# Where the Mish of eight held chunks stands in ScalarE's queue, in a fused attention and two-layer MoE kernel

## The chip, the cores and the metric

The kernel runs on one core of a Trainium2 chip. The metric is the device time of one execution in microseconds: 1049.36 as the median of three runs (1048.75 to 1050.46). Everything below is read from one profiled execution of that kernel. Five engines work side by side, each with its own queue that it takes in order: TensorE (PE, with its weight loads as PEld), VectorE (DVE), ScalarE (ACT), GpSimd (POOL) and SyncE (SP), which issues the loads from memory.

## The reference

Three stages follow each other over 1152 tokens of width 512:

```
attn_out = softmax over 144 means of 4 positions (repeated 4 times) + softmax over a band of +-3 positions
x  = attn_out as [1152, 512]
h  = x @ w_in                      # 512 -> 2048
g  = h * tanh(log1p(exp(h)))       # Mish
x  = g @ w_out                     # 2048 -> 512
P  = exp(x @ w_gate - max), 8 rounds of row and column normalisation
out = sum over 8 experts of P[:, e] * (relu(x @ w1[e]) @ w2[e])
```

The change touches only the Mish of the second stage. All matmuls that matter are done as three products of rounded operands (high x high, low x high, high x low), so that every operand is first split into a rounded part and a rest.

## The kernel before, in words

The middle stage is cut into chunks. A chunk is 128 of the 2048 hidden columns for one of three groups of 384 tokens. `gemm1(s)` (L500) computes chunk s into a PSUM bank with 12 matmuls; `mish(s, hps)` (L489) then does three things: ACT applies Mish in place (L495), ACT copies the result rounded into `ghi` or a slot of `xform` (L496), and DVE subtracts to get the rest, `glo` (L497). `gemm2(s)` (L513) multiplies both by `w_out` with 12 matmuls, four chunks later (`LAG = 4`).

Eight of the chunks are computed early. While attention still runs, the first tokens are ready and PE has gaps; there `p_gemm1` (L931) puts the first matmuls of the eight chunks named in `HELD` (L942), and `hold` copies each result out of PSUM to a tile `ghi` or `glo` in SBUF (L953 on DVE, L955 on ACT). These chunks wait there; in the main loop (L1025) they are the numbers s = 6 to 9 (tiles `glo`) and 12 to 15 (tiles `ghi`). At their turn the loop does not call `gemm1` but `mish` alone (L1037 and L1038).

Three things set the order of the queues. In attention a planner (`Plan`) lays out the steps by a table of costs, and `pin` (L567) ties each instruction to the one ahead of it on its engine. The loop is traced after that; a scheduler places its instructions on each engine as early as its own timing allows, unless `tc.issue_after(x)` holds them back: what is traced inside such a block is queued behind x, if it is on x's engine. `last["pe"]` is the last matmul of the plan, `last["mish"]` the newest ACT copy (L496, or L855 in attention). Before the change the loop's `issue_after(last["pe"])` holds back only the work on PE. The Mish of a held chunk needs nothing but its SBUF tile, so nothing holds it back on ACT.

ACT evaluates functions from a loaded table, and Exp (attention, L721) and Mish (L495) are in different ones; an ACT_TABLE_LOAD stands wherever the queue goes from one to the other.

Other steps that the text names: L654 turns queries and keys on PE, L667 copies them on ACT; L745 and L810 are scores, L713 their maxima on DVE, L721 the exponentials on ACT, L727 to L731 the scaling on DVE, L763 and L828 transposes on PE with copies L766 and L830 on ACT, L781 and L838 the products with the values, L788 and L844 their joining, L855 and L857 the split of the result. Weights come as 64-bit numbers: loaded by SP (L436, L872), turned into 32 bits by ACT (L453, L891) and three steps on DVE (L454 to L457, L895 to L904), split by ACT (L463) and POOL (L464).

Of the kernel before, what the change touches and what calls it, by code (L numbers as in the profile page):

```python
# [325 lines left out]
def attn_moe_moe_kernel(  # L326
# [44 lines left out]
    def f32(a):  # L371
        return a.bitcast(F32)

    def new(pool, shape, dt, tag, bufs=2):
        return pool.tile(shape, dt, tag=tag, name=tag, bufs=bufs)
# [29 lines left out]
    def bank(tag):  # L405
        turn[tag] += 1
        return of_tag[tag][turn[tag] % 4]

    last = {}
# [30 lines left out]
    def w_raw():  # L440

        n, i = divmod(place["raw"], 2)
        if n >= len(ring) or n >= place["split"] + RAWB:
            return
        place["raw"] += 1
        if i == 0:
            wraw[n] = raw_place(n % RAWB)
        w = raw64.pop((n, i)).rearrange("p (n t) -> p n t", t=2)  # L450
        c = slice(512 * i, 512 * i + 512)
        lo, hi, x = w[:, :, 0], w[:, :, 1], wraw[n].bitcast(U32)[:, c]
        ACT.activation(out=f32(x), in_=f32(hi), func=AF.Copy, scale=F64_BIAS)  # L453
        DVE.tensor_scalar(out=x, in0=x, scalar1=3, scalar2=0x7FFFFFF8, op0=ALU.logical_shift_left,  # L454
                          op1=ALU.bitwise_and)
        DVE.scalar_tensor_tensor(out=x, in0=hi, scalar=0x80000000, in1=x, op0=ALU.bitwise_and, op1=ALU.bitwise_or)
        DVE.scalar_tensor_tensor(out=x, in0=lo, scalar=29, in1=x, op0=ALU.logical_shift_right, op1=ALU.bitwise_or)  # L457
        load_w64()
# [7 lines left out]
    def w_split():  # L466

        n = place["split"]
        place["split"] += 1
        kind, j = ring[n]  # L470
        hi, lo = (new(ap, [128, 1024], F32R, f"{z}{kind}", NBUF) for z in ("hi", "lo"))
        split(wraw.pop(n), hi, lo)
        whl[kind, j] = hi, lo

    def free_at(n):

        kind, j = ring[n]
        before = [x for k, x in ring[:n] if k == kind]
        if len(before) < NBUF:
            return 0  # L480
        return 2 * lasts[kind, before[-NBUF]] + 2 + (LAG if kind == 2 else 0)
# [6 lines left out]
    gq, acc, ysum, gl, held = {}, {}, {}, {}, {}  # L488
    def mish(s, hps):  # L489

        if s < SWITCH:
            ghi, glo = (xform[:, s % (LAG + 1), z].rearrange("p a b -> p (a b)")[:, 0:NMAX] for z in range(2))
        else:
            ghi, glo = (new(ap, [128, NMAX], F32R, z, LAG) for z in ("ghi", "glo"))
        ACT.activation(out=hps, in_=hps, func=AF.Mish)  # L495
        last["mish"] = ACT.activation(out=ghi, in_=hps, func=AF.Copy)  # L496
        DVE.tensor_tensor(out=glo, in0=hps, in1=f32(ghi), op=ALU.subtract)  # L497
        gq[s] = ghi, glo

    def gemm1(s):  # L500
        g, j, h, _, _ = chunks[s]
        n, c0 = groups[g][1] * TQ, groups[g][0] * TQ
        bk = bank("w")[:, 0:n]
        whi, wlo = (z.rearrange("p (a b) -> p a b", a=KD) for z in whl[1, j])
        o = slice(128 * h, 128 * h + 128)
        i = 0
        for kk in range(KD):
            for a, b in ((whi, xhi), (whi, xlo), (wlo, xhi)):
                PE.matmul(out=bk, lhsT=a[:, kk, o], rhs=b[:, kk, c0:c0 + n], start=(i == 0), stop=(i == 3 * KD - 1))  # L509
                i += 1  # L510
        mish(s, bk)

    def gemm2(s):  # L513
        g, j, h, first, end = chunks[s]
        n, c0 = groups[g][1] * TQ, groups[g][0] * TQ
        whi, wlo = (z.rearrange("p (a b) -> p a b", a=2) for z in whl[2, j])
        ghi, glo = gq.pop(s)
        done = end and s // 2 == last_of[g]
        joined = g in ysum
        if end and not joined:  # L520
            ysum[g] = room(g)
        for d in range(KD):
            if first:
                acc[d] = bank("acc")
            bk = acc[d][:, 0:n]
            o = slice(128 * d, 128 * d + 128)
            for i, (a, b) in enumerate(((whi, ghi), (whi, glo), (wlo, ghi))):
                PE.matmul(out=bk, lhsT=a[:, h, o], rhs=b, start=(first and i == 0), stop=(end and i == 2))  # L528
            if not end:
                continue  # L530
            z = ysum[g][d][:, 0:n]
            if not joined:
                ACT.activation(out=z, in_=bk, func=AF.Copy)
            elif not done:
                DVE.tensor_tensor(out=z, in0=bk, in1=z, op=ALU.add)
            else:
                y = xs[d // KH][:, d % KH, c0:c0 + n]
                DVE.tensor_tensor(out=y, in0=bk, in1=z, op=ALU.add)
                parts(y, xhi[:, d, c0:c0 + n], xlo[:, d, c0:c0 + n])
# [10 lines left out]
    def gate():  # L550

        gl["w"] = wghl = tp.tile([128, KD, 128], F32R, name="wghl")
        SP.dma_start(out=wg, in_=w_gate.rearrange("(a p) e -> p a e", p=128))
        ACT.activation(out=wghl, in_=ident.unsqueeze(1).to_broadcast([128, KD, 128]), func=AF.Copy, scale=0.0)
        ACT.activation(out=wghl[:, :, 0:NE], in_=wg, func=AF.Copy)
        DVE.tensor_tensor(out=wghl[:, :, NE:2 * NE], in0=wg, in1=f32(wghl[:, :, 0:NE]), op=ALU.subtract)
# [468 lines left out]
    for s in range(S0):  # L1025
        if s == S0 - 1:
            with tc.issue_after(last["mish"].ins):
                gate()
        n = place["raw"] // 2
        if n < len(ring) and s >= need[ring[n]] - AHEAD and (s % 2 == 0 or s >= need[ring[n]] - 4):  # L1030
            with tc.issue_after(last["mish"].ins):
                w_raw()
        n = place["split"]
        if n < len(ring) and 2 * n + 2 <= place["raw"] and free_at(n) <= s:
            w_split()
        with tc.issue_after(last["pe"]):
            if s in held:  # L1037
                mish(s, held.pop(s))  # L1038
            else:
                gemm1(s)  # L1040
            if s >= LAG:
                gemm2(s - LAG)

# [595 lines left out]
```

## Time and profile before

| | |
|---|---|
| median of three runs | 1049.36 us |
| the profiled execution | 1048.87 us |
| its span, from first to last instruction | 1046.9 us |
| PE busy | 1026.5 us, 98% of the span |
| DVE busy | 694.5 us, 66% |
| ACT busy | 536.0 us, 51% |
| POOL busy | 391.9 us, 37% |
| attention with the held chunks | from 0 to 120.66 us |
| main loop | from 120.66 us to about 263 us |
| last stage | from there to the end |

The shares are means over stages that have different limits. A timeline row begins with the start and the duration of a piece of work, and ends in brackets with how long its engine had been idle and what ended that. A row of the chain of waits is a piece of the path that was last to end.

### The profile page before, as it was taken

How to read it: one execution, taken by the hardware profiler on the slowest of the kernel's cores; microseconds unless marked ns; L12 is line 12 of the kernel's file. 1: busy time of each engine (PE TensorE's matmuls, PEld its weight loads, DVE VectorE, ACT ScalarE, POOL GpSimd, SP SyncE). 2: the span in 40 equal slices, each digit the busy share in tenths (PEclk: the TensorE clock that was granted, in tenths of full speed). 3: DMA queues.
4: the chain of work that ended last, by engine and by line, in shares of the span. 5: the costliest groups of instructions: out<-in, count | busy, mean ns of one | idle time of the engine just before them, and what ended most of it. 6: DMA issues, size and time to landing. Idle time of an engine off the chain costs nothing.

```text
span 1046.9 us, 17277 instructions
## 1 busy us (share of the span) xinstructions
PE 1026.5 (98%) x6376; PEld 933.8 (89%) x6376; DVE 694.5 (66%) x1338; ACT 536.0 (51%) x1365; POOL 391.9 (37%) x435
## 2 busy tenths in 40 slices
PE   8988899999999999999999999999999999999998
PEld 6876799999999888988998899989998999889997
DVE  6876654434478988776665776586756677657844
ACT  6999854434358544544553445435553455345531
POOL 0111122103045437744453444435452455244530
PEclk9998999999999999999999999999999999999999
DMA  9552222212003011201111012101110121011002
GB/s 220 162 129 66 70 91 100 91 72 71 1 1 121 22 50 61 61 2 59 61 61 32 29 61 61 54 8 61 61 61 1 61 61 61 14 48 61 21 1 91
DMA packets 47996, 63.40 MB, mean 61 GB/s; under 512 B 15272, under 2 KB 31656, under 8 KB 47912
## 3 DMA queue, kind: packets, MB, share of 16 engines
q1 hardware_dynamic: 47912, 62.30, 20.0%
q8 instruction: 50, 0.82, 0.3%
q14 instruction: 34, 0.28, 0.1%
HBM read 59.93 MB, written 2.36 MB: 59 GB/s over the span
## 4 chain that ended last, share of the span: by engine, by line
PE 90%; ACT 7%; DMA 2%; DVE 1%; issue 0%; DVEq 0%; ACTq 0%
PE bank L1554 38%; PE bank L1502 30%; PE bank L528 7%; PE bank L509 6%; PE bank L1179 2%; ACT pl L721 2%; PE bank L1161 2%; DMA raw<-in_moe_w_out_dram 1%; ACT pg L721 1%; ACT L495 1%; ACT L721 1%; PE bank L1334 1%; DMA rawq<-in_k_dram 0%; PE bank L654 0%; PE bank L1343 0%; PE bank L781 0%
## 5 line engine op out<-in xcount | busy, mean ns | idle before, releaser
L1517 ACT ACTIVATE xs<-bank 128x384 f32<-128x384 f32 x231 | 113.2, 492 | 258.1 <-PE bank L1502 238.5
L1554 PE MATMUL bank<-xs,hhi 128*128 128x512 f32 x760 | 235.7, 391 | 0.0
L1570 DVE SCALAR_TENSOR_TENSOR yacc<-bank,P,yacc 128x512 f32<-128x512 f32 (+1 forms) x217 | 161.0, 746 | 94.3 <-PE bank L1554 92.4
L1554 PEld LDWEIGHTS bank<-xs,hhi 128*128 128x128 f32 x760 | 140.5, 188 | 19.6
L1554 PE MATMUL bank<-xs,hlo 128*128 128x512 f32 x380 | 148.9, 392 | 0.0
L1477 POOL TENSOR_TENSOR wops<-wsums,wops 128x256 fp32r<-128x256 f32 x114 | 85.8, 762 | 163.2 <-ACT wops L1475 163.0
L1244 DVE TENSOR_TENSOR bank<-bank,xs 128x384 f32<-128x384 f32 x189 | 99.0, 559 | 45.7 <-ACT xs L1517 37.3
L1554 PE MATMUL bank<-wc,hhi 128*128 128x512 f32 x398 | 123.0, 390 | 0.0
L1502 PE MATMUL bank<-xform,wops 128*128 128x384 f32 x558 | 106.2, 335 | 0.0
L1502 PEld LDWEIGHTS bank<-xform,wops 128*128 128x128 f32 x558 | 98.0, 188 | 4.4
L464 POOL TENSOR_TENSOR lo<-raws,hi 128x512 fp32r<-128x512 f32 x26 | 34.3, 1327 | 167.8 <-ACT hi L463 154.9
L1322 DVE SCALAR_TENSOR_TENSOR hlo<-bank,hhi 128x384 fp32r<-128x384 f32 x150 | 78.8, 550 | 16.3 <-ACT hhi L1319 14.0
L1319 ACT ACTIVATE hhi<-bank 128x384 fp32r<-128x384 f32 x150 | 70.4, 487 | 37.1 <-DVE bank L1244 31.5
L1554 PEld LDWEIGHTS bank<-wc,hhi 128*128 128x128 f32 x398 | 74.5, 188 | 15.6
L1244 DVE TENSOR_TENSOR wsums<-raws 128x256 f32<-128x256 f32 x147 | 64.1, 448 | 35.4 <-POOL wops L1477 17.4
L1554 PEld LDWEIGHTS bank<-xs,hlo 128*128 128x128 f32 x380 | 71.3, 188 | 16.2
L1554 PE MATMUL bank<-wc,hlo 128*128 128x512 f32 x199 | 78.2, 393 | 0.0
L1477 POOL TENSOR_TENSOR ysum<-wsums,ysum 128x256 fp32r<-128x256 f32 x59 | 45.5, 777 | 81.3 <-ACT ysum L1475 81.2
L1502 PE MATMUL bank<-xhi,wops 128*128 128x384 f32 x252 | 70.8, 336 | 0.3 <-ACT xs L1517 0.3
L1475 ACT ACTIVATE wops<-wsums 128x256 fp32r<-128x256 f32 x114 | 45.3, 411 | 34.9 <-PE bank L1502 27.7
L1364 POOL TENSOR_TENSOR xs<-temp,xs 128x512 fp32r<-128x512 f32 x42 | 58.0, 1402 | 9.9 <-ACT xs L1362 9.9
L1502 PE MATMUL bank<-xform,ysum 128*128 128x384 f32 x282 | 54.9, 336 | 0.0
(237 smaller groups left out, 2185.6 us busy)
## 6 DMA issues: line engine op xcount, KB each, us to landing
temp<-in_moe_w_dram SPq DMA_DIRECT2D x64, 256.0 KB, 3.1
raws<-in_moe_w_dram SPq DMA_DIRECT2D x16, 768.0 KB, 4.5
raw<-in_moe_w_in_dram SPq DMA_DIRECT2D x16, 512.0 KB, 6.7
raw<-in_moe_w_out_dram SPq DMA_DIRECT2D x16, 512.0 KB, 3.2
raws<-in_moe_w_dram SPq DMA_DIRECT2D x5, 512.0 KB
rawq<-in_q_dram SPq DMA_DIRECT2D x4, 576.0 KB, 10.1
rawv<-in_v_dram SPq DMA_DIRECT2D x8, 288.0 KB
vw<-in_v_dram SPq DMA_DIRECT2D x12, 192.0 KB, 4.2
```

Of the source, the lines that this page charges most:

```text
L509: PE.matmul(out=bk, lhsT=a[:, kk, o], rhs=b[:, kk, c0:c0 + n], start=(i == 0), stop=(i == 3 * KD - 1))
L528: PE.matmul(out=bk, lhsT=a[:, h, o], rhs=b, start=(first and i == 0), stop=(end and i == 2))
L1244: eng.tensor_tensor(out=out, in0=a, in1=b, op=ALU.add if cb > 0 else ALU.subtract)
L1319: ACT.activation(out=hb.t[0], in_=bk.t[:, 0:TH], func=AF.Relu)
L1322: DVE.scalar_tensor_tensor(out=hb.t[1], in0=bk.t[:, 0:TH], scalar=0.0, in1=f32(hb.t[0]), op0=ALU.max, op1=ALU.subtract)
L1364: add("wlo", lambda raw=raw, y=y: POOL.tensor_tensor(out=y.t[:, 1], in0=raw(), in1=f32(y.t[:, 0]), op=ALU.subtract), r=[("r2", c), ("ch", ...
L1475: add("wh", lambda src=src, y=y: ACT.activation(out=y.t[:, 0], in_=piece(src), func=AF.Copy), r=key + rk, w=[("wh", r, n)] + wk, b=[y] + bs)
L1477: add("wl", lambda src=src, y=y: POOL.tensor_tensor(out=y.t[:, 1], in0=piece(src), in1=f32(y.t[:, 0]), op=ALU.subtract), r=key + [("wh", r ...
L1502: PE.matmul(out=bb.t[:, 0:TH], lhsT=y.t[:, wz, kk, :], rhs=x[xz][:, kk, :], start=(fresh and i == 0), stop=(i == 3 * KH - 1), skip_group_c ...
L1517: add("keep", lambda src=src, y=y: ACT.activation(out=y.t, in_=src.t[:, 0:TH], func=AF.Copy), r=[key, "late"], w=[("b", id(y))], b=[src, y])
L1554: PE.matmul(out=bk.t[:, a:b], lhsT=h[hz][:, js], rhs=y[:, wz, a:b], start=(f == fs[0] and i == 0), stop=(f == fs[-1] and i == 2))
L1570: DVE.scalar_tensor_tensor(out=y, in0=bk.t[:, a:b], scalar=p, in1=y, op0=ALU.mult, op1=ALU.add)
```

## The change

Inside the loop, the `mish` of a held chunk gets an `issue_after` of its own, on the copy (L496) of the chunk traced before it. The branches are swapped; what is computed stays.

```
         with tc.issue_after(last["pe"]):
-            if s in held:
-                mish(s, held.pop(s))
+            if s not in held:
+                gemm1(s)
             else:
-                gemm1(s)
+                with tc.issue_after(last["mish"].ins):
+                    mish(s, held.pop(s))
             if s >= LAG:
                 gemm2(s - LAG)
```

The queues of PE, DVE, POOL and SP keep their order, instruction for instruction. ACT's changes in three kinds of places. The first is in attention, at the exponentials L721 (tiles `pl` near, `pg` far); `ghi` is a held chunk:

```order
 L891 ACTIVATE raws<-raw_991 128x512
-L495 ACT_TABLE_LOAD
-L495 ACTIVATE ghi<-ghi 128x384
-L721 ACT_TABLE_LOAD
 L721 ACTIVATE pl_101,ld<-bank_115,lm 96x102 x4
 L721 ACTIVATE pg_103,gd<-bank_111,gm 72x144 x2
 L721 ACTIVATE pg_104,gd<-bank_117,gm 72x144 x2
-L495 ACT_TABLE_LOAD
-L495 ACTIVATE ghi<-ghi 128x384
-L721 ACT_TABLE_LOAD
```

A held Mish leaves, and with it the load of its table and the load of the exponentials' table behind it. In all, eleven loads leave attention with the eight Mishes: eight with the four `ghi`, two with the first `glo` and one with the second, behind which no exponential follows.

The second is the head of the loop on ACT, behind the last split of attention's result (L855):

```order
-L495 ACTIVATE glo<-glo 128x384
 L855 ACTIVATE xhi<-bank_112 128x4x96
 L453 ACTIVATE raws<-raw_1593 128x512
 L463 ACTIVATE hi_1776<-raws 128x512
+L495 ACT_TABLE_LOAD
 L495 ACTIVATE bank_113<-bank_113 128x384
 L496 ACTIVATE xform<-bank_113 128x384
```

One load now stands ahead of the loop's first Mish, that of chunk 0, and it takes over that Mish's wait for the matmuls of chunk 0.

The third is at the held chunks' turn in the loop, here s = 6 to 9 (the same again for 12 to 15, on `ghi`):

```order
 L453 ACTIVATE raws<-raw_1774 128x512
-L496 ACTIVATE xform<-glo 128x384 x2
+L495 ACTIVATE glo<-glo 128x384
+L496 ACTIVATE xform<-glo 128x384
+L495 ACTIVATE glo<-glo 128x384
+L496 ACTIVATE xform<-glo 128x384
 L463 ACTIVATE hi_1878<-raws 128x512
 L453 ACTIVATE raws<-raw_1816 128x512
```

Each held Mish now stands directly ahead of the copy that reads it.

## Rows read from the trace of the kernel before

**Rows 1.** The page's part 4: shares of the chain that ended last.

```profile
PE 90%; ACT 7%; DMA 2%; DVE 1%; issue 0%; DVEq 0%; ACTq 0%
```

**Rows 2.** Busy time by stretch: PE, PEld, DVE, ACT, POOL, clock, DMA.

```profile
66.74:90.80 24.06, 16.40 (x211) 12.73 (x207) 14.15 (x43) 23.84 (x66) 0.00 (x0) 0.96 0.07 16
90.80:97.00 6.20, 6.20 (x67) 5.62 (x68) 2.19 (x6) 5.08 (x20) 1.27 (x1) 0.60 0.30 89
97.00:120.66 23.66, 19.86 (x220) 16.84 (x217) 18.28 (x41) 22.36 (x76) 3.72 (x3) 1.00 0.24 68
120.66:135.60 14.94, 14.94 (x85) 14.82 (x86) 8.57 (x15) 8.17 (x16) 4.25 (x4) 1.00 0.33 111
```

**Rows 3.** Lines L495 and L721: ns min/median/max, first and last start.

```profile
L495 ACT ACT_TABLE_LOAD  x6: 1283/1283/1283, 67.4 to 111.9; - x6
L495 ACT ACTIVATE ghi<-ghi x4: 523/524/527, 68.7 to 88.1; 128x384 f32<-128x384 f32 x4
L495 ACT ACTIVATE glo<-glo x4: 507/523/542, 103.7 to 119.7; 128x384 f32<-128x384 f32 x4
...
L721 ACT ACT_TABLE_LOAD  x5: 1283/1283/1283, 69.3 to 104.3; - x5
```

**Rows 4.** Chain of waits, 66 to 122: start us, us, what.

```profile
67.44 1.28 ACT L495
68.73 0.53 ACT ghi L495
69.26 1.28 ACT L721
```

**Rows 5.** Timeline of PE: where it waited in attention's second half.

```profile
72.01 0.45 PE L942 MATMUL bank<-xhi,hi 128*128 128x384 f32 x1 [1.87 <-ACT pl L721]
...
88.84 0.46 PE L803 MATMUL bank<-maskb,identb 96*96 96x408 bf16 x1 [1.67 <-ACT odT L788]
90.80 0.88 PE L828 MATMUL bank<-ident,pl 96*102 96x96 f32 x4 [1.50 <-ACT odT L788]
...
114.19 1.64 PE L838 MATMUL bank<-pt,vw 102*64 102x96 f32 x30 [1.44 <-ACT pt L830]
...
120.66 0.80 PE L509 MATMUL bank<-xhi,hi 128*128 128x384 f32 x3 [1.77 <-ACT xhi L855]
```

**Rows 6.** Chain of waits: the same PE work at both clock levels.

```profile
36.48 0.88 PE bank L810 x16
...
37.84 1.47 PE bank L838 x32
39.31 0.47 PE bank L828 x4
...
91.68 1.61 PE bank L810 x16
93.29 2.68 PE bank L838 x32
```

**Rows 7.** Timeline of DVE: maxima (L713) and the last weight step's start.

```profile
67.45 0.58 DVE L713 TENSOR_REDUCE lm<-bank 96x4 f32<-96x408 f32 x1 [0.71 <-PE bank L810]
...
104.40 2.04 DVE L713 TENSOR_REDUCE lm<-bank 96x4 f32<-96x408 f32 x4
...
116.05 0.43 DVE L895 TENSOR_SCALAR raws<-raws 128x512 uint32<-128x512 uint32 x1 [0.31 <-ACT raws L891]
```

**Rows 8.** Timeline of ACT: an exponential after a switch, and the loop.

```profile
105.57 0.34 ACT L721 ACTIVATE pl<-bank,lm 96x102 f32<-96x102 f32 x1
...
125.40 0.47 ACT L495 ACTIVATE bank<-bank 128x384 f32<-128x384 f32 x1 [0.74 <-PE bank L509]
...
127.48 0.47 ACT L495 ACTIVATE bank<-bank 128x384 f32<-128x384 f32 x1 [0.53 <-PE bank L509]
...
141.87 0.53 ACT L496 ACTIVATE xform<-glo 128x384 fp32r<-128x384 f32 x1 [0.48 <-PE bank L528]
```

**Rows 9.** Chain of waits: the first `gemm2` in the loop.

```profile
131.43 2.08 PE bank L528 x12
```

## Prediction

> **What bounds the kernel now.** I read the shares of the chain of waits first: 90% of the path that ended last is PE, 7% is ACT [rows 1]. So almost anywhere a faster ACT is worth nothing, and the question is where its 7% lie. Next the busy time by stretch. From 120.66 us on PE is busy without a gap (14.94 of 14.94 us in the first stretch of the loop), and ACT only 8.17 of it; between 66.74 and 120.66 it is the other way round: ACT is busy 23.84 of 24.06 us while PE is busy 16.40, and later 22.36 of 23.66 against 19.86 [rows 2]. There ACT sets the pace. Then the source view of the two lines that load tables: eleven loads of 1.283 us and eight Mishes of about 0.52, all between 67.4 and 119.7 us [rows 3], and the chain of waits runs through them one after the other [rows 4]. Last the timeline of PE, for what it waits for there: exponentials, copies and splits on ACT, in waits of 1.4 to 1.9 us [rows 5].
>
> **The change part by part.** All sums are made against the profiled execution, 1048.87 us with a span of 1046.9; it lies 0.49 below the median of the runs, and I take what I find off the median.
>
> *What leaves ACT's queue in attention:* 11 x 1.283 = 14.1 us of loads and 8 x 0.52 = 4.2 us of Mish, 18.3 us together. Two loads with the Mish between them fill 67.44 to 70.54 without a gap, 1.28 + 0.53 + 1.28 [rows 4], so a load costs its own length and nothing around it. That is ACT's sum and not yet time: PE and DVE keep their order and work, so I walk the stretches and ask what is late next.
>
> *First stretch, 66.74 to 90.80.* Eight loads and the four `ghi` Mishes lie here: 10.3 + 2.1 = 12.4 us of ACT. PE was idle for 24.06 - 16.40 = 7.66 us [rows 2]. The first exponentials can start when DVE has their maxima, 67.45 + 0.58 = 68.03 [rows 7], 2.5 us earlier than behind the second load. From there each thing that PE waited for is ready before PE comes to it: the bank that L942 wanted is free after four exponentials of about 0.34 us [rows 8], at about 69.5, while PE's work ahead of it lasts until 72.01 - 1.87 = 70.14 [rows 5], so that wait goes; the copies L788, for which PE waited 1.67 and 1.50 [rows 5], lose a Mish and two loads directly ahead of them. ACT gives up more than PE can use, so PE becomes the bound and the 7.66 are the ceiling. I take 7.3, the ceiling less a few hand-offs; the lower end is half the ceiling, 3.8, if DVE, busy 14.15 of the 24.06 and in series with ACT in every softmax, takes over half of the waits.
>
> *Clock, 90.80 to 97.00.* The granted clock is 0.60 of full here and PE has no gap [rows 2]: it runs the first part at the lower of its two levels, 1.2 GHz, after the waits of 1.67 and 1.50 us with little work between. The same work elsewhere at 2.4 GHz shows the price: L810 0.88 against 1.61, L838 1.47 against 2.68 [rows 6], L828 0.47 [rows 6] against 0.88 [rows 5], together 2.82 against 5.17, so 2.35 us. With the waits ahead of it gone I take 2.3. If the clock falls nevertheless, it is 0. Worse than nothing is excluded, since PE's work gets denser.
>
> *Second stretch, 97.00 to 120.66.* Two loads and a Mish stand ahead of the exponentials at 105.57 [rows 8]. But DVE gives the first of their four maxima only at 104.40 + 0.5 = 104.9 [rows 7], and DVE does not wait for ACT there, so 0.6 to 0.7 us come off, not 3.1. The load and the Mish near 112 stand ahead of the copies L830 for which PE waited 1.44 [rows 5]: 1.28 + 0.5 = 1.8 come off whole. Behind that, ACT's conversion L891 releases DVE at 116.05 [rows 7], and from there a chain on DVE, 4.6 us up to the loop's first matmul at 120.66, keeps its length; the last two Mishes stand beside it and give nothing. So 0.6 + 1.8 = 2.4 us. Bounds: 0.6 if the copies are late for another reason, 23.66 - 19.86 = 3.8 if PE's idle time goes altogether [rows 2].
>
> *What is added in the loop.* One load ahead of the first Mish. It waits for chunk 0's matmuls, so it does not hide behind them: the Mish, its copy and the DVE step come 1.28 us later, and queued behind them are the next Mishes and the weight conversions. ACT then has idle time of 0.74 and 0.53 us ahead of the second and third chunks' Mishes [rows 8], 1.27 together, and is back in time at 127.5. PE first asks for such a result at 131.43 [rows 9]. Cost 0; without that cover 1.28.
>
> *The eight Mishes in the loop.* Each stands ahead of a copy that waits for PE to free its slot; the shortest of the eight idle times there is 0.48 us [rows 8], against a Mish of 0.52. So at most 0.04 us of lateness, four chunks before PE uses the result. Cost 0; without that cover 8 x 0.52 = 4.2. The other queues keep their order, and the loads that SP issues depend on buffers that DVE frees, so they move earlier with the work; nothing in the loop is tied to a fixed moment.
>
> Sum: 7.3 + 2.3 + 2.4 = 12.0 us off, 1049.36 - 12.0 = 1037.4 us. From the bounds: at least 3.8 + 0 + 0.6 = 4.4, at most 7.66 + 2.35 + 3.8 = 13.8, that is 1035.6 to 1045.0.
>
> *A rule weighed against the rows.* My ceiling uses PE's busy time. Its weight loads are busy for less: 12.73 and 16.84 us in the two stretches against 16.40 and 19.86 [rows 2]. The Trainium skill (Perfetto Trace Analysis, section Identifying the Most-Contended Engine) says that matmul busy time is a poor measure of TensorE's headroom, and that the busy share of weight loads is to be read. By that the ceiling would be 11.3 + 6.8 us instead of 7.66 + 3.8. This trace leaves it open: in the dense loop both numbers are alike, 14.94 and 14.82 [rows 2], but attention's many small matmuls are not like that loop.
>
> **The rivals.**
>
> *The whole of ACT's sum comes off.* If PE's busy time in attention is mostly the tails of small matmuls, PE is no bound and 18.3 us go: 1049.36 - 18.3 = 1031.1. For it: the chain runs through every load. Against it: DVE's maxima at 104.9 and the chain from 116.05 on, which do not depend on ACT's switches. This is where the rule of the Trainium skill above would lead.
>
> *DVE and PE hand the waits to each other.* In each softmax ACT, DVE and PE alternate, and the order was laid out for other durations; half of the first stretch's gain, half of the clock's and 1 us of the second give 3.8 + 1.2 + 1.0 = 6.0: 1043.4. For it: DVE is busy 18.28 of 23.66 us in the second stretch [rows 2]. Against it: in the first it is busy only 14.15 of 24.06.
>
> *Nothing moves.* The tie changes ACT's queue but the end of attention is set by DVE and the weights: 1049.4. Against it: PE's waits name ACT [rows 5].
>
> *Slower.* ACT in the loop gets 4.2 us of Mish and 1.28 us of load in front of the weight conversions; if ACT's lead over PE there is less than that, PE waits for the late results: 1049.36 + 5.5 = 1054.9. It decides from the point at which the idle time ahead of the held chunks' copies is clearly shorter than a Mish, and only if attention gives nothing back. For it: 0.48 is already just under 0.52. Against it: ACT is idle for 6.8 us of the loop's first 14.94 [rows 2], and PE uses a result four chunks later.
>
> **How the numbers follow.** Forecast, 9.5 to 13.8 us off: 0.70. Hand-over, 4.4 to 9.5: 0.16. Whole sum: 0.08. Nothing: 0.02. Slower: 0.04. A difference below 0.2% (2.1 us) can't be told from none for this kernel; so faster 0.94, same 0.02, slower 0.04. The forecast's own range is 1035.6 to 1039.9. The whole range goes down to 1034.5, a part of the way to the larger gain, and up to 1042.0, which takes in the better half of the hand-over; what is left out is about 0.06 of the whole sum below, 0.08 of the hand-over and the 0.06 of the last two cases above, 0.2 together.
>
> **What would show it.** In the profile after: one table load at L495 instead of six and none at L721; PE's idle time between 66 us and the loop's start down from 11.5 us to about 2 to 3, and that little in the last 10 us; the granted clock at full level over the whole of attention; the loop's first matmul L509 at about 108.7 instead of 120.66; the wait ahead of the exponentials in the second stretch now on DVE's maxima; and from there on PE without a gap for the same length as before, with all of the gain there and nothing lost later. Wrong would be: new waits of PE for ACT in the loop, a low clock in attention, or waits on weights (`raw` loads, POOL's L464) at the loop's start, where the loads have less time.

## The result and the profile after

The changed kernel takes 1034.33 us as the median of four runs (1034.09 to 1034.44), the kernel before, with one run more than the three above, 1049.91 (1048.75 to 1051.01): a ratio of 0.9851 with a 95% interval of 0.9834 to 0.9869. Forecast were 1037.4 and a range of 1034.5 to 1042.0; the direction was right, and the time lies 0.2 us below the range. The profiled executions are 1048.87 and 1034.31 us, 14.56 apart, with spans of 1046.9 and 1032.4. Of the difference of the medians, 15.58, the remaining 1.0 is that the profiled execution of before was one of its shorter ones.

ACT's share of the chain that ended last has gone from 7% [rows 1] to 2%, and the page's part 4 of the kernel after begins so:

```profile
PE 94%; DVE 3%; ACT 2%; DMA 1%; issue 0%; SPq 0%; DVEq 0%
```

PE now carries nearly all of it, and DVE has come up from 1% to 3%. The source view of L495 after (count, ns min/median/max, first and last start) answers to rows 3:

```profile
L495 ACT ACTIVATE glo<-glo x4: 509/516/522, 122.4 to 127.7; 128x384 f32<-128x384 f32 x4
L495 ACT ACTIVATE ghi<-ghi x4: 508/508/509, 139.1 to 144.4; 128x384 f32<-128x384 f32 x4
...
L495 ACT ACT_TABLE_LOAD  x1: 1283/1283/1283, 109.1 to 109.1; - x1
```

One load of L495 is left, at the head of the loop, and the eight held Mishes run between 122.4 and 145 us, beside dense PE work. L721 has no load left.

To see where the time went I cut both traces at the same four matmuls of PE: the scores L810 x16 near 66 us, the last four transposes L828 x4 ahead of the next L810 x16, the products L838 x16 behind that, and the loop's first matmul L509. Busy time by stretch, first before, then after, columns as in rows 2:

```profile
66.48:90.80 24.32, 16.66 (x212) 12.99 (x211) 14.41 (x43) 23.84 (x66) 0.00 (x0) 0.96 0.08 18
90.80:97.48 6.68, 6.68 (x70) 5.83 (x71) 2.67 (x7) 5.56 (x21) 1.27 (x1) 0.63 0.32 93
97.48:120.66 23.18, 19.38 (x214) 16.64 (x213) 17.80 (x39) 21.88 (x74) 3.72 (x3) 1.00 0.23 67
```

```profile
65.92:80.80 14.88, 14.88 (x212) 12.85 (x211) 14.20 (x43) 12.19 (x56) 0.00 (x0) 1.00 0.20 29
80.80:85.56 4.76, 4.50 (x71) 3.76 (x69) 3.98 (x11) 4.76 (x20) 1.27 (x1) 1.00 0.55 162
85.56:106.04 20.48, 18.73 (x214) 16.39 (x213) 17.36 (x37) 16.43 (x67) 3.42 (x3) 1.00 0.29 78
106.04:120.98 14.94, 14.94 (x86) 14.82 (x87) 8.48 (x15) 9.32 (x17) 4.06 (x4) 1.00 0.37 105
```

| piece | before | after | off | forecast |
|---|---|---|---|---|
| start to the first mark | 66.48 | 65.92 | 0.56 | none |
| first stretch | 24.32 | 14.88 | 9.44 | 7.3 |
| clock stretch | 6.68 | 4.76 | 1.92 | 2.3 |
| second stretch | 23.18 | 20.48 | 2.70 | 2.4 |
| loop's first matmul to the end of the span | 926.24 | 926.36 | -0.12 | 0 |

The four pieces make 14.62 at the loop's start. In the first stretch PE is busy for all of its 14.88 us; the clock is at its full level of 2.4 GHz in all four stretches; ACT, which had been busy 23.84 of 24.32 us, is busy 12.19 of 14.88. The 0.56 ahead of the first mark is chance: no instruction differs there, and nine other profiles of this study with the same work ahead of it reach that mark between 65.60 and 66.68, with ACT's old order and the new one mixed. Of PE's five waits in rows 5 only the last is left. All that PE waited for between 60 and 150 us after the change:

```profile
PE bank L509 <- ACT xhi L855: 1.7, 1, 1.7
PE bank L586 <- ACT pt L830: 0.3, 1, 0.3
```

### The profile page after: what moved, and what is told of

It reads as the page before. It is cut to its first block, busy times and chain, and to the rows that moved or that the text cites. A ratio compares the mean times of both kernels' runs of the same rounds, so it can differ in the third digit from the quotient of the medians.

```text
span 1032.4 us, 17281 instructions
## 1 busy us (share of the span) xinstructions
PE 1021.9 (99%) x6376; PEld 931.4 (90%) x6376; DVE 695.2 (67%) x1338; ACT 522.8 (51%) x1355; POOL 392.0 (38%) x435
## 4 chain that ended last, share of the span: by engine, by line
PE 94%; DVE 3%; ACT 2%; DMA 1%; issue 0%; SPq 0%; DVEq 0%
PE bank L1555 38%; PE bank L1503 31%; PE bank L528 7%; PE bank L509 7%; PE bank L1180 2%; PE bank L1162 2%; ACT pl L721 1%; PE bank L654 1%; PE bank L781 1%; PE bank L942 1%; DMA rawq<-in_q_dram 1%; PE bank L828 1%; PE bank L1335 1%; PE bank L810 1%; PE bank L838 1%; PE bank L1344 0%
## 5 line engine op out<-in xcount | busy, mean ns | idle before, releaser
L1555 PEld LDWEIGHTS bank<-wc,hhi 128*128 128x128 f32 x398 | 74.5, 188 | 15.6
```

The source lines that it names most:

```text
L1555: PE.matmul(out=bk.t[:, a:b], lhsT=h[hz][:, js], rhs=y[:, wz, a:b], start=(f == fs[0] and i == 0), stop=(f == fs[-1] and i == 2))
```

## The experiments

Eleven kernels were run in three series, each on another chip: experiments 1 to 4, 5 to 8 and 9 to 11. The kernel before has a median of 1049.38 in the first, 1049.91 in the second and 1049.75 in the third. The ratios to it are those of the runs taken together and not quotients of the medians.

**1. The loads or the Mishes?** In the kernel before, the held chunks' Mish is replaced by a copy in place, which needs no other table: the eight instructions stay where they were in attention, the loads go.

```
-    def mish(s, hps):
+    def mish(s, hps, fn=AF.Mish):
...
-        ACT.activation(out=hps, in_=hps, func=AF.Mish)
+        ACT.activation(out=hps, in_=hps, func=fn)
...
-                mish(s, held.pop(s))
+                mish(s, held.pop(s), AF.Copy)
```

> The kernel before, with the Mish of the eight held chunks replaced by a plain copy at the same place in ACT's queue: the Mish of those chunks is left out, the eight instructions and their durations stay, the ten extra table loads go. Theory (the loads count, and once they are gone PE sets the pace of 66 to 81 us, with 14.7 us of work against 12.1 + 2.1 = 14.2 on ACT): nearly the whole gain, 1034.5 to 1036. Rival A (time follows ACT's sum): 14.1 of 18.3 us, so 77% of the 15.6, 1037.9. Rival B (the Mishes count, not the loads): above 1045.

Measured 1035.61 (1034.58 to 1036.57), ratio 0.9859 [0.9835, 0.9883]. The source view of L495 shows eight activations still in attention and one load behind it:

```profile
L495 ACT ACTIVATE ghi<-ghi x4: 510/533/612, 67.7 to 78.9; 128x384 f32<-128x384 f32 x4
L495 ACT ACTIVATE glo<-glo x4: 507/568/600, 90.5 to 105.7; 128x384 f32<-128x384 f32 x4
L495 ACT ACT_TABLE_LOAD  x1: 1283/1283/1283, 109.7 to 109.7; - x1
```

The first two stretches are those of the changed kernel, 65.86 to 80.91 (15.05) and 80.91 to 85.67 (4.76). The loop begins 40.76 us behind the first mark, against 40.12 after and 40.24 in experiment 10, which runs the changed kernel again. So the eleven loads, 14.1 us of ACT, were the price; the 4.2 us of activations beside them cost 0.5 to 0.6 once ACT has slack.

**2. and 3. One half alone.** Only the four `ghi` (s = 12 to 15) are tied, or only the four `glo` (s = 6 to 9). The condition of the new branch gets `s >= 12` or `s < 12`; the others keep the old call.

```
-            else:
+            elif s >= 12:          # experiment 3: s < 12
                 with tc.issue_after(last["mish"].ins):
                     mish(s, held.pop(s))
+            else:
+                mish(s, held.pop(s))
```

> Only the four held chunks s = 12 to 15 (tiles ghi) are tied; the four glo Mishes stay in attention. Theory: the first stretch (9.3) and the clock (2.1) come off, and the 0.6 that PE gained ahead of the stretch if that is more than chance: 1037.9 to 1038.5. Rival A (ACT's sum: 12.4 of 18.3): 1039.3.

> Only the four held chunks s = 6 to 9 (tiles glo) are tied; the four ghi Mishes with their eight loads stay. Theory: only the second stretch changes, 2.7 us off, 1047.2; PE still waits 1.5 to 1.9 us for ACT near 72 and 89 and the clock falls near 90. Rival A (ACT's sum: 3 loads and 4 Mishes, 5.9 of 18.3): 1044.9. This run also shows whether PE waits 0.5 us at L803 near 65 us as in before, ahead of every moved instruction.

Measured 1038.58 (1036.97 to 1039.56), ratio 0.9886 [0.9862, 0.9911], for `ghi`, and 1047.87 (1046.84 to 1048.82), ratio 0.9981 [0.9970, 0.9993], for `glo`: 10.8 and 1.5 us off, 12.3 together, against 14.1 to 15.6 for both at once (runs 10 and after). The stretches of experiment 3, columns as in rows 2, show its half in the second one:

```profile
65.70:90.95 25.25, 17.86 (x212) 14.44 (x211) 15.11 (x44) 24.14 (x67) 0.00 (x0) 0.92 0.12 21
98.20:118.56 20.36, 18.63 (x214) 16.39 (x213) 17.24 (x37) 16.40 (x67) 3.38 (x3) 1.00 0.24 69
```

The second stretch is 20.36 us, as after (20.48), 2.8 less than before; the clock still falls near 90, as expected, and the clock stretch between the two rows is 7.25 us in this profile. With `ghi` alone the first stretch is as after (66.02 to 80.90), and PE's timeline in the second shows the wait for `pt` of rows 5 with a price:

```profile
102.43 2.82 PE L838 MATMUL bank<-pt,vw 102*64 102x96 f32 x30 [1.44 <-ACT pt L830]
```

The same 30 matmuls took 1.64 us behind the same wait of 1.44 in the kernel before [rows 5]; here they take 2.82, because the clock falls: it is at 0.50 from 103 to 108 us. The runs of experiment 2 part by the clock: 1039.56 at a mean of 0.997, 1036.97 at 0.999. That the first half brings this fall on is not shown: in experiment 6, where all eight Mishes are still in attention, the clock fell behind the same wait too (0.50 at 116 to 118 us). Nor is it clear of the noise that the halves do not add up: 1.8 to 3.3 us are missing, and the interval of experiment 2 alone is 2.6 wide to either side.

**4. One Mish left behind.** The changed kernel with one of the eight, s = 15, left at its old place: two loads and one Mish, 3.1 us of ACT.

```
-            else:
+            elif s != 15:
                 with tc.issue_after(last["mish"].ins):
                     mish(s, held.pop(s))
+            else:
+                mish(s, held.pop(s))
```

> All held chunks are tied but s = 15: one Mish with two loads, 3.1 us of ACT, stays in the first stretch. Theory (PE sets the pace there and ACT has 14.7 - 12.1 = 2.6 us to spare): 0.5 to 1.5 us slower than the change, 1035 to 1036, the clock stays at full. Rival A (each us of ACT is a us): 1037.4. Rival C (one such wait is enough to let the clock fall): another 2 us, 1039.5.

Measured 1038.54 (1038.04 to 1039.07), ratio 0.9886 [0.9859, 0.9913]. That is 4.2 us above the changed kernel's 1034.33 and 2.9 above its 1035.65 in experiment 10, for 3.1 us of ACT; my theory, that slack hides most of it, fell. The times alone do not part the two rivals. The profile does, since the clock falls in it: the loop begins 43.77 us behind the first mark instead of 40.12, and of the 3.65 us the first stretch has 2.16, the clock stretch 1.25 and the second 0.24. PE's timeline, then the clock (the column behind POOL's) in windows of 2 us:

```profile
82.64 0.54 PE L828 MATMUL bank<-ident,pl 96*102 96x96 f32 x4 [1.62 <-ACT odT L788]
83.11 1.68 PE L810 MATMUL bank<-kT,qT 64*96 64x102 f32 x16
84.72 2.41 PE L838 MATMUL bank<-pt,vw 102*64 102x96 f32 x32
```

```profile
82.00:84.00 2.00, 1.36 (x14) 1.24 (x16) 0.00 (x0) 2.00 (x8) 0.00 (x0) 0.79 0.82 266
84.00:86.00 2.00, 2.00 (x26) 1.81 (x26) 1.07 (x2) 2.00 (x11) 0.23 (x1) 0.50 0.04 8
```

A wait of 1.62 us, with little work ahead of it, and the clock goes to half, 1.2 GHz; L810 and L838 take 1.68 and 2.41 us, where the changed kernel's take 0.94 and 1.54. So one switch back and forth cost its wait and the clock behind it.

**5. and 6. Is PE alone the pace of the first stretch?** Twelve of the held chunks' matmuls (four of the twelve for each of three chunks, 2.1 us of PE) are left out, once in the changed kernel and once in the kernel before.

```
-        bk, z = Buf(RB, "gemm1"), wbuf[1, j]
+        bk, z, at = Buf(RB, "gemm1"), wbuf[1, j], len(held)
...
+                if part == 1 and at in (1, 2, 3):
+                    continue
```

> The changed kernel, in which the second, third and fourth held chunk leave out four of their twelve matmuls (12 of L942, 0.174 us each, 2.1 us of PE, most of it between 66 and 81 us). Theory (PE sets the pace there now): 1.5 to 2.1 us faster than the change, 1032.3 to 1032.8. Rival (ACT or DVE still sets it): 1034.3.

> The kernel before, with the same 12 matmuls left out. Theory (ACT sets the pace there): within 0.5 us of before, about 1049.5. Rival (PE's work counts there as well): 2.1 us faster, 1047.8.

Measured 1034.76 (1033.80 to 1035.27), ratio 0.9855 [0.9834, 0.9876], for the changed kernel without them, and 1049.81 (1048.52 to 1050.39), ratio 0.9991 [0.9975, 1.0006], for the one before. In the kernel before, PE has slack and nothing comes off, as expected. In the changed one the loop begins at 105.20 us instead of 106.04. Four of the twelve matmuls lie ahead of the first mark, which is reached 0.64 us earlier. Eight, 1.4 us, lie in the first stretch, and there the theory held by a third only: it is 14.44 us instead of 14.88. Of the sum, 0.24 goes again in the clock stretch, behind a longer wait for `pt` (0.49 instead of 0.26). The row of the first stretch says why so little came:

```profile
65.28:79.72 14.44, 13.91 (x204) 11.42 (x203) 14.34 (x45) 12.32 (x56) 0.00 (x0) 1.00 0.22 38
```

DVE is busy for 14.34 of the 14.44 us; it was already at 14.20 of 14.88 in the changed kernel. PE is the bound there by 0.5 us only, and DVE is next. This is read from busy times; no run takes work from DVE there, and the one wait that PE has, 0.53 us, ends with ACT's copy L766. The median does not show the 0.84 because the clock falls at the loop's head in this profile, for 1.55 us (see experiment 10).

**7. DVE's chain ahead of the loop.** After the change the loop's first matmul still waits 1.72 us, for a split behind DVE work. In the changed kernel the three DVE steps of the last weight conversion in the plan, and the load that needs their buffer, are laid behind attention. The lines that mark these steps as `last` are left out below.

```
+            if getattr(x, "last", False):
+                back.append((x, new))
+                continue
...
+        for x, new in back:
+            for z, ring, i in new:
+                z.t = ring.make(i)
+            self.emit(x.fn)
```

> The changed kernel, in which the last weight conversion that the plan places in attention (three DVE steps, L895 to L904, about 1.6 us, and the load that waits for them) comes behind attention's last step on DVE. Theory (the 1.7 us that PE still waits at the loop's start hang on that chain; next in line is PE's own last product with the values): the loop's first matmul 0.6 to 0.8 us earlier, 1033.6. Rival (the weights of the loop come late for it): PE waits in the loop, 1034.3 or more.

Measured 1033.43 (1033.27 to 1034.52), ratio 0.9845 [0.9824, 0.9866]. The profiled execution was the longest of the five, and its loop began at 106.24, no earlier than after. Counted from the first mark, which chance puts late here (66.68), it is 39.56 us against 40.12, and the wait at the loop's start is 1.19 instead of 1.72. Run 11 repeats it beside the changed kernel.

**8. and 9. The price of the clock by itself.** In the kernel before, with ACT's order untouched, 17 more matmuls that add zeros are put where PE waited near 89 and 91 us [rows 5]. In the first form they use 32 rows of PE, in the second 128; what they stream differs too, the mask in the first and the identity in the second.

```
+                for _ in range((9, 8)[par] if t == 9 else 0):
+                    PE.matmul(out=view(bks[0].t), lhsT=identb[:32, 32:128],
+                              rhs=maskb[:32, m0:m0 + W].unsqueeze(1).to_broadcast([32, 4, W]), start=False, stop=False)
```

```
+    zerob = at.tile([128, 96], BF16, name="zerob", bufs=1)
...
+    DVE.memset(zerob, 0.0)
...
+                    PE.matmul(out=view(bks[0].t), lhsT=zerob,
+                              rhs=identb[:, 0:W].unsqueeze(1).to_broadcast([128, 4, W]), start=False, stop=False)
```

> The kernel before, with 17 extra matmuls that add zeros to an open group, in PE's queue at its two waits near 89 and 90 us (9 and 8 of 0.17 us). No wait is taken away. Theory (the clock is a term of its own): the granted clock stays at full near 91 to 95 us and 1.5 to 2.1 us come off, 1047.8 to 1048.4. Rival (the work at the lower clock lay beside a wait anyway): full clock and no change, 1049.9. If the extra work is longer than the waits: up to 0.5 us slower.

> The kernel before, with the order of ACT untouched: 17 extra matmuls of 128 rows by 96 columns by 408 with zero weights are added to the mask group ahead of the scores L810 that were slow (9 and 8 of them, about 0.17 us each at full clock, 2.9 us in waits of 1.67 + 1.50 us), so that PE works where it waited. My theory (PE's waits with little work let the clock fall, and the fall costs 2.1 us): the granted clock stays at 1.00 between 88 and 97, L810 takes 0.88 and L838 1.47 us, and the time is about 2 us below that of the kernel before, 1047.5 to 1048.2. Rival 1 (work of this kind does not hold the clock): 0.5 to 0.6 in 88 to 96 as in the filler of 32 rows, and 1050.5 to 1051.7. Rival 2 (the clock holds, but ACT's switches set the end of this stretch in any case): clock 1.00, loop start within 0.5 us of 120.7, 1049.9.

Measured 1051.56 (1049.51 to 1054.23), ratio 1.0010 [0.9993, 1.0027], with 32 rows, and 1049.34 (1048.15 to 1050.24), ratio 0.9984 [0.9969, 0.9999], with 128. The clock in the same stretch, with 32 rows:

```profile
86.00:88.00 2.00, 2.00 (x16) 1.33 (x15) 1.60 (x6) 1.97 (x5) 0.00 (x0) 1.00 0.00 0
88.00:90.00 2.00, 2.00 (x8) 0.95 (x7) 1.03 (x3) 1.97 (x5) 0.00 (x0) 0.72 0.10 35
90.00:92.00 2.00, 2.00 (x8) 1.08 (x7) 0.00 (x0) 1.99 (x7) 0.00 (x0) 0.50 0.60 231
92.00:94.00 2.00, 2.00 (x21) 1.57 (x21) 0.00 (x0) 1.56 (x7) 1.26 (x1) 0.50 0.04 8
```

and with 128 rows, with the timeline of PE behind it:

```profile
90.00:92.00 2.00, 1.76 (x15) 1.05 (x15) 0.00 (x0) 1.99 (x7) 0.00 (x0) 1.00 0.58 174
92.00:94.00 2.00, 2.00 (x47) 1.90 (x46) 1.11 (x3) 2.00 (x9) 0.96 (x1) 1.00 0.27 100
```

```profile
91.36 0.54 PE L833 MATMUL bank<-ident,pl 96*102 96x96 f32 x4 [0.24 <-ACT odT L790]
91.83 0.94 PE L815 MATMUL bank<-kT,qT 64*96 64x102 f32 x16
92.70 1.56 PE L843 MATMUL bank<-pt,vw 102*64 102x96 f32 x32
```

With 32 rows PE is busy without a gap and the clock falls all the same. With 128 rows it holds in the profiled execution: L810 (here L815) takes 0.94 us and L838 (here L843) 1.56, against 1.68 and 2.41 in experiment 4, and the clock stretch is 5.21 us (91.36 to 96.57) instead of 6.68. So 1.5 us come off for the clock alone, with ACT's order as before. The first stretch is 25.15 us instead of 24.32, but the fillers are not the cause: from ACT's first table load to L828 it is 23.38 us (67.98 to 91.36), as in experiment 3 (67.57 to 90.95), which has no fillers, and 23.36 before (67.44 to 90.80). ACT began 0.54 us later, behind a longer wait for a weight load, here before and then experiment 9:

```profile
66.74 0.68 ACT L891 ACTIVATE raws<-raw 128x512 f32<-128x512 f32 x1 [0.72 <-DMA raw<-in_moe_w_out_dram]
```

```profile
67.29 0.67 ACT L896 ACTIVATE raws<-raw 128x512 f32<-128x512 f32 x1 [1.33 <-DMA raw<-in_moe_w_out_dram]
```

In the profiled execution, 1048.15, 0.7 is left against 1048.87. The medians are 0.4 apart, and the interval of the ratio nearly reaches 1; the theory expected 2. So the clock's price is shown in the stretch and not in the time of the run. Most of the other executions have a mean granted clock of 0.995 instead of the profiled one's 0.999, so in them it fell somewhere; where, no profile shows.

**10. and 11. The changed kernel again, beside experiment 7.** No edit to either.

> The changed kernel once more, as the yardstick of the next run. Theory: 1034.3 again, within 0.3. If its few runs so far fell on one of two levels, then some at about 1033.3.

> The changed kernel with the DVE steps of the last weight conversion in the plan, and the load that waits for them, put behind attention, once more beside the changed kernel on the same chip. Theory (DVE's chain sets the start of the loop, so that 0.9 us come off): 1033.4, below the changed kernel's by 0.6 to 1.2, and in the profile the loop's first matmul at about 105.1 instead of 106.04. Rival (the 0.9 between runs on different chips is chance): within 0.3 us of the changed kernel, and the loop's first matmul at 106.0 to 106.3.

Measured 1035.65 (1035.57 to 1035.70), ratio 0.9853 [0.9831, 0.9876], for the changed kernel, and 1033.91 (1033.30 to 1035.11), ratio 0.9837 [0.9814, 0.9860], with the conversion laid behind. Every run of the second is faster than the fastest of the first. The changed kernel is 1.3 us slower here than in the result, outside what I expected. Its profile gets to the loop at the same point (105.84, after the same wait of 1.73), and then the clock falls. Windows of the changed kernel in the result, then in this run:

```profile
106.00:108.00 2.00, 1.96 (x11) 1.84 (x12) 1.90 (x4) 0.55 (x1) 0.54 (x1) 1.00 0.55 215
108.00:110.00 2.00, 2.00 (x13) 2.00 (x12) 0.47 (x1) 1.48 (x2) 0.79 (x1) 1.00 0.15 41
```

```profile
106.00:108.00 2.00, 2.00 (x10) 1.88 (x11) 1.93 (x4) 0.35 (x1) 0.34 (x1) 0.80 0.43 172
108.00:110.00 2.00, 2.00 (x8) 2.00 (x7) 0.26 (x1) 0.81 (x2) 1.00 (x1) 0.50 0.39 57
```

From the first L509 to the first L528 PE needs 12.16 us instead of 10.60: that is the 1.5. Experiments 1, 4 and 5 paid it too, in their profiles (12.18, 12.14 and 12.15 us). In experiment 1 the runs part by it: 1036.33 and 1036.57 at a mean clock of 0.998, 1034.58 and 1034.88 at 1.000. Three of the four runs of experiment 10 have a mean clock of 0.998; the fourth has 1.000 and took as long, and what slowed that one is not known. In the profile with the conversion laid behind, the wait is shorter and the clock holds:

```profile
105.66 0.80 PE L517 MATMUL bank<-xhi,hi 128*128 128x384 f32 x3 [1.19 <-ACT xhi L863]
```

From L810's mark to the loop's start it is 39.55 us, against 40.24 in experiment 10 and 40.12 in the result. So the theory on DVE's chain holds with 0.6 to 0.7 us instead of the 0.9 that I gave it; the other 1.1 of the 1.74 between the two medians fits the clock's fall at the loop's head, roughly. This is the fastest version of the study.

## Why the prediction was right, and where its size was off

*What leaves ACT in attention: right.* All eleven loads are gone and one is new. That the loads and not the Mishes are the price is shown by experiment 1.

*First stretch: the step that failed.* I took 7.66 us, the stretch less PE's busy time, as the ceiling, and 7.3 of it. It gave 9.44, so the ceiling itself was false. The 212 matmuls that were busy for 16.66 us in the kernel before are busy for 14.88 after; 7.66 us of idle time and 1.78 us of busy time went, 9.44 together. The view by line (busy us, mean ns, idle us and its releasers) shows where, before:

```profile
L828 PE MATMUL bank<-ident,pl 96*102 96x96 f32 x13 | 1.8, 265 | 2.2 <-ACT odT L788 1.5 <-ACT pg L721 0.7
L763 PE MATMUL bank<-ident,pg 72*72 72x72 f32 x16 | 1.6, 228 | 1.1 <-ACT qT L667 1.1
L781 PE MATMUL bank<-pt,vd 72*64 72x72 f32 x32 | 1.5, 232 | 0.0
...
L803 PE MATMUL bank<-maskb,identb 96*96 96x408 bf16 x2 | 0.8, 396 | 1.7 <-ACT odT L788 1.7
```

and after:

```profile
L828 PE MATMUL bank<-ident,pl 96*102 96x96 f32 x13 | 1.4, 249 | 0.0
L763 PE MATMUL bank<-ident,pg 72*72 72x72 f32 x16 | 1.3, 225 | 0.0
L781 PE MATMUL bank<-pt,vd 72*64 72x72 f32 x32 | 1.2, 229 | 0.0
...
L803 PE MATMUL bank<-maskb,identb 96*96 96x408 bf16 x2 | 0.5, 340 | 0.0
```

These four lines alone fall from 5.7 to 4.4 us, with the same counts and, but for L803, nearly the same length of one matmul. In front of a wait or a small hitch a matmul's whole length counts as busy, and in dense work the next one lies over most of it. The two matmuls of L803 show it. Before, one stands ahead of a wait of 1.67 us and the other, at 88.84, ahead of one of 1.50 [rows 5], and they count 0.8 us; after, with 0.34 us each, they reach from 80.44 to the next matmul at 80.80 and count 0.36:

```profile
80.44 0.52 PE L803 MATMUL bank<-maskb,identb 96*96 96x408 bf16 x2
```

About 0.1 of it is the lower clock, at which the one at 88.84 took 0.46. Set side by side in the two traces, 14 of the stretch's 212 matmuls make up 1.7 of the 1.78 us, and the five largest pieces, 0.16 to 0.28 us each, belong to matmuls directly ahead of a wait. So the busy time of a stretch with many waits is no floor for it.

The rule weighed there (the Trainium skill, Perfetto Trace Analysis, Identifying the Most-Contended Engine) calls matmul busy time a bad measure of headroom, and this trace agrees, by 1.78 us. The busy time of weight loads, which it names in its place beside the share of peak arithmetic, is no floor here either: it is 12.99 us before and 12.85 after, which made the ceiling 11.3. The stretch ended at 14.88, between 16.66 and 12.99. And PE is not the only limit there: DVE is busy 14.20 us of it, and with less work on PE the stretch went down by 0.44 us only (experiment 5).

*How far luck has a part.* Forecast and profiled execution are 3.0 us apart. The first stretch is 2.1 of it; 0.56 is the chance ahead of the first mark, and 0.49 comes from taking the sum off a median that lay above the profiled execution; the errors of the other terms, -0.4 and 0.3, nearly cancel. So chance alone is larger than the 0.2 us by which the time left the range, and experiment 10 has the same kernel at 1035.65, inside it. That the first stretch went below PE's busy time of 16.66 us, which I had taken for its floor, is no chance: it is 14.88 after and 15.05, 14.88 and 15.00 in experiments 1, 2 and 10.

*Clock: right for this stretch.* 2.3 was forecast and 1.92 came: PE's busy time there falls by 2.18, from 6.68 to 4.50, and a new wait of 0.26 for `pt` is in it. That the fall has a price of its own, apart from ACT's switches, is shown in the profile of experiment 9 (1.5 us), and that one switch was enough to bring it on in experiment 4. "Worse than nothing is excluded" did not hold for the kernel as a whole: in experiment 10 the clock fell at the loop's head, where it had held in the kernel before, and cost 1.56 us. It fell there in four of the eight profiles without the loads of the `ghi` in attention, or with those of one (experiments 1, 4, 5 and 10), and in none of the five others; why is open. That nothing but the waits decides whether it falls is not shown; see the last section.

*Second stretch: right, in both terms.* The exponentials come 0.8 us earlier in the stretch (105.57 - 97.48 = 8.09 before, 92.84 - 85.56 = 7.28 after), where 0.6 to 0.7 was forecast, and they now wait for DVE's maxima, as ACT's timeline has it:

```profile
92.84 0.34 ACT L721 ACTIVATE pl<-bank,lm 96x102 f32<-96x102 f32 x1 [2.29 <-DVE lm L713]
```

The other 1.9 us, where 1.8 was forecast, come behind the exponentials. The forecast took ACT's 1.8 whole although PE's wait for `pt` was only 1.44 [rows 5]. Counted on PE, nearly all of the 2.70 us are that wait, one of 0.53 for `pl` at 107.99 that the prediction did not list, and 0.65 of busy time, which falls from 19.38 to 18.73 as it did in the first stretch. The clock has no part in it: it was at 1.00 there before, too. The last two Mishes gave nothing, as said; the wait ahead of L509 is 1.72 instead of 1.77.

*Added load in the loop, and the eight Mishes there: cost 0, right.* ACT's timeline at the loop's head and at the held chunks' turn:

```profile
109.15 1.28 ACT L495 ACT_TABLE_LOAD   x1
110.44 0.47 ACT L495 ACTIVATE bank<-bank 128x384 f32<-128x384 f32 x1
...
111.34 0.49 ACT L495 ACTIVATE bank<-bank 128x384 f32<-128x384 f32 x1
...
112.85 0.47 ACT L495 ACTIVATE bank<-bank 128x384 f32<-128x384 f32 x1
...
122.45 0.52 ACT L495 ACTIVATE glo<-glo 128x384 f32<-128x384 f32 x1
123.14 0.53 ACT L496 ACTIVATE xform<-glo 128x384 fp32r<-128x384 f32 x1 [0.17 <-PE bank L528]
...
125.22 0.53 ACT L496 ACTIVATE xform<-glo 128x384 fp32r<-128x384 f32 x1 [1.14 <-PE bank L528]
```

Counted from the loop's first matmul, the first Mish is 1.4 us late (110.44 - 106.04 = 4.40 against 123.65 - 120.66 = 2.99), the second 0.6, and the third is at 6.81 against 6.82 [rows 8]: the lateness is used up where the prediction had it. Seven of the eight held copies still wait for PE, the first two 0.17 and 1.14 us, so the Mishes ahead of them lie in idle time. PE waits for neither.

*The rivals.* The whole of ACT's 18.3 us did not come: ACT's idle time ahead of the exponentials shows DVE next. Its condition, that busy time is tails of small matmuls, was true for 1.78 of 16.66 us in the first stretch. Hand-over, 6.0 us, was less than half of it. Slower needed waits in the loop, and there is none.

## What to carry to other kernels

An activation whose function is in another table than its neighbours' cost two loads here wherever its neighbours' kind came on both sides, 2.57 us beside its own 0.52; work that is ready early should be held back until its own kind is at hand. The ceiling of a stretch with many waits is its length less what the same instructions take in dense work, not less their busy time among the waits. When one engine becomes free, look for the second in line and for waits that are left: here DVE was about 0.5 us behind PE in the first stretch, and moving one conversion off its chain ahead of the loop gave 0.6 to 0.7 us more.

## What the runs showed of the hardware

TensorE's clock fell while PE was busy without a gap. In experiment 8 PE was busy for 2.00 of 2.00 us from 86 us on, with matmuls of 32 rows filling the waits, and the clock went from 1.00 to 0.50 near 88.9; in the profiled execution of experiment 9, with matmuls of 128 rows and the same columns, it stayed at 1.00.

Where ACT set the pace, a fall cost no time. In experiment 3 the clock was low from 73.3 to 76.7 us too, which it was not in the kernel before; ACT sets the pace there, and from its first load to L828 it took 23.38 us against 23.36.

The length of a wait alone does not tell whether it falls. The clock fell behind waits of 1.44 (experiments 2 and 6), 1.62 (experiment 4) and 1.73 us (experiment 10); it held behind 1.87 us at 72.01 and 1.44 at 114.19 in the kernel before [rows 5], and behind 1.72 at the loop's start after the change. The same kernel with the same wait there did both, in two executions. What else decides stays open.

A table load took 1.283 us in every one of its instances here and left nothing behind it: 67.44 + 1.28 is 68.72, and the Mish began at 68.73 [rows 4].
